# Decode kernel bound by its loads: load targets placed first in SBUF, other packet sizes, x on a second queue, one output store

## The chip, the cores and the metric

The kernel runs on one core of a Trainium2 chip; the other cores are idle. The metric is device time in microseconds (us), the median of several executions. The profile is one execution taken by the hardware profiler; its span, from the first to the last instruction, is some 1.8 us shorter than the time. SyncE and SP are the same engine, as are ScalarE and ACT, VectorE and DVE, TensorE and PE, GpSimd and POOL.

## The reference, cut to what matters

A decode step for 4 sequences: layer norm of x, an attention block over a window of 2048 cached keys and 16 key-value heads, and beside it an MLP; all are added up.

```python
xn  = layernorm(x)                                  # x: 4 x 1 x 576, bf16
q   = xn @ wq                                       # wq: 576 x 4096
o   = softmax(q @ K[window].T * 128**-0.5) @ V[window]   # K, V: 4 x 16 x 8192 x 128
out = x + o @ wo + B(xn)                            # wo: 4096 x 576
# B: x1 + gelu(layernorm(x1) @ w3) @ w4             # w3: 576 x 4608, w4: 4608 x 576
# (with one token the shifts of the first half of B give zeros, so x1 is xn; w1 and w2 are not read)
```

Only the window of K and V and the four weights have to be read: 87.17 MB. Nearly every byte is used once.

## The kernel before: what the change and the argument touch

Pools are laid out in SBUF in the order in which they are opened. All small tiles come first, the load targets after them:

```python
    const = ctx.enter_context(tc.tile_pool(name="const", bufs=1))
    small = ctx.enter_context(tc.tile_pool(name="small", bufs=2))
    kvp = ctx.enter_context(tc.tile_pool(name="kv", bufs=NKV))      # 7 tiles of 16 KB per partition, K and V
    ...                                                            # kt, pt
    wp = ctx.enter_context(tc.tile_pool(name="w", bufs=1))          # wq, then w3, then w4
    wop = ctx.enter_context(tc.tile_pool(name="wo", bufs=2))
```

The first loads, all on SyncE's queue:

```python
    x_bf = const.tile([B, D], BF16)
    nc.sync.dma_start(out=x_bf[:], in_=x2)
    wq_main = A_wq[0:KJ * P, :].rearrange("(p j) n -> p j n", j=KJ)
    for j in range(KJ):                                            # 4 DMAs, packets of 8 KB
        nc.sync.dma_start(out=wq_sb[:, j * NQ:(j + 1) * NQ], in_=wq_main[:, j, :])
```

The last load is w4, in pieces of 9, 9, 9, 5 and 4 rows per partition (a row is 1152 bytes). Everything is summed in one PSUM tile `acc`: the 576 output columns are cut in four blocks of 144, block i on partitions 32i to 32i+3 (in the code B = 4 sequences, NQD = 4 blocks, CW = 144 columns, QD = 32 partitions, D = 576, and for w4 NF = 36 rows per partition, NFH = 18). The end:

```python
    def acc_matmuls(lhsT, rhs):                                    # lhsT has 4 columns
        for i in range(NQD):
            nc.tensor.matmul(out=acc[i * QD:i * QD + B, :], lhsT=lhsT, rhs=rhs[:, i * CW:(i + 1) * CW], ...)
    ...
    fin = const.tile([P, CW], out.dtype)
    nc.vector.tensor_copy(out=fin[:], in_=acc[:])
    for i in range(NQD):
        eng = nc.sync if i % 2 == 0 else nc.scalar
        eng.dma_start(out=o2[:, i * CW:(i + 1) * CW], in_=fin[i * QD:i * QD + B, :])
```

## Time and profile before

| | before |
|---|---|
| time, median | 216.15 us (216.03 to 216.25, 3 runs) |
| span of the profile | 214.6 us |
| load queue, share of 16 DMA engines | 95.7% |
| first wq packet starts | 2.15 us |
| last data packet ends | 209.82 us |
| typical 16384-byte packet | 611 ns |

The last three rows come from the trace's record of single DMA packets (start, duration, size, queue); such numbers are called "packet records" below. They don't name the DMA engine.

From the page of the kernel before: PE's busy time, the granted TensorE clock, DMA share and rate in 40 slices of the span, and the load queue (q1) and the queue of instruction fetches (q8) with packets, MB and share of 16 engines.

```profile
PE 121.0 (56%) x2893; PEld 94.9 (44%) x2893; DVE 118.0 (55%) x223; ACT 70.1 (33%) x258; POOL 6.1 (3%) x14
PEclk9999999999999999999999999999999999999995
DMA  5999999999999999999999999999999999999960
GB/s 207 429 437 434 428 429 425 425 425 437 426 429 423 437 431 419 439 425 434 431 428 425 428 428 430 422 434 431 429 418 428 437 419 425 437 427 422 419 262 12
q1 hardware_dynamic: 7080, 87.17, 95.7%
q8 instruction: 22, 0.36, 0.6%
```

No compute engine is busy for more than 56% of the span, while DMA is at 9 tenths or more from the second slice to the 38th. The time is the stream of loads, plus what comes before its first and after its last packet. The last pieces of the chain of waits (start, duration, what) say so too: a load of w4, then the matmuls that need it, then the copy of the result.

```profile
182.78 27.43 DMA w_sb<-in_B_w_dram
210.26 0.68 PE acc L247 x16
```

The two ends in the timeline (start, duration, engine and line, operation, count, idle time before it and what ended it). At the start SyncE issues x, then wq:

```profile
0.73 0.36 SPq L87 DMA_DIRECT2D x_bf<-in_A_x_dram  x1
1.16 2.06 SPq L92 DMA_DIRECT2D wq_sb<-in_A_wq_dram  x4
...
210.26 0.65 PE L247 MATMUL acc<-w_sb,gT 128*4 128x144 bf16 x16 [0.61 <-DMA w_sb<-in_B_w_dram]
...
210.96 0.31 DVE L480 CAST fin<-acc 128x144 bf16<-128x144 f32 x1 [5.87 <-PE acc L247]
211.29 0.63 SPq L483 DMA_DIRECT2D out_dram<-fin  x2
211.30 0.92 ACTq L483 DMA_DIRECT2D out_dram<-fin  x2
```

### The profile page before, as it was taken

How to read it: one execution, taken by the hardware profiler on the slowest of the kernel's cores; microseconds unless marked ns; L12 is line 12 of the kernel's file. 1: busy time of each engine (PE TensorE's matmuls, PEld its weight loads, DVE VectorE, ACT ScalarE, POOL GpSimd, SP SyncE). 2: the span in 40 equal slices, each digit the busy share in tenths (PEclk: the TensorE clock that was granted, in tenths of full speed). 3: DMA queues.
4: the chain of work that ended last, by engine and by line, in shares of the span. 5: the costliest groups of instructions: out<-in, count | busy, mean ns of one | idle time of the engine just before them, and what ended most of it. 6: DMA issues, size and time to landing. Idle time of an engine off the chain costs nothing. (4 is left out here: it accounts for less than half of the span.)

```text
span 214.6 us, 6449 instructions
## 1 busy us (share of the span) xinstructions
PE 121.0 (56%) x2893; PEld 94.9 (44%) x2893; DVE 118.0 (55%) x223; ACT 70.1 (33%) x258; POOL 6.1 (3%) x14
## 2 busy tenths in 40 slices
PE   0461355647470017157999577677474705779752
PEld 0350143445360015145899456555453604557641
DVE  5608799766470047348610798785573924854210
ACT  0000005571634001607070045570725340709600
POOL 5400100000000000000000000000000000000000
PEclk9999999999999999999999999999999999999995
DMA  5999999999999999999999999999999999999960
GB/s 207 429 437 434 428 429 425 425 425 437 426 429 423 437 431 419 439 425 434 431 428 425 428 428 430 422 434 431 429 418 428 437 419 425 437 427 422 419 262 12
DMA packets 7123, 87.58 MB, mean 408 GB/s; under 512 B 820, under 2 KB 824, under 8 KB 1336
## 3 DMA queue, kind: packets, MB, share of 16 engines
q1 hardware_dynamic: 7080, 87.17, 95.7%
q8 instruction: 22, 0.36, 0.6%
q14 instruction: 5, 0.04, 0.0%
q10 hardware_dynamic: 16, 0.00, 0.0%
HBM read 87.17 MB, written 0.00 MB: 406 GB/s over the span
## 5 line engine op out<-in xcount | busy, mean ns | idle before, releaser
L302 ACT ACTIVATE pt<-S 32x128 bf16<-32x128 f32 x256 | 68.5, 268 | 92.0 <-issue 55.3
L259 DVE STREAM_TRANSPOSE kt<-kn 128x1024 int32<-128x1024 int32 x64 | 74.3, 1205 | 11.4 <-DMA kn<-in_A_k_cache_dram 11.4
L313 PE MATMUL O<-pt,vn 128*128 128x8 bf16 x1024 | 37.4, 169 | 43.2 <-DMA vn<-in_A_v_cache_dram 41.7
L313 PEld LDWEIGHTS <-vn 128*128 128x128 bf16 x1024 | 34.4, 105 | 51.3 <-DMA vn<-in_A_v_cache_dram 43.6
L273 PE MATMUL S<-qz,kt 128*128 128x32 bf16 x1024 | 39.1, 189 | 25.2 <-DVE kt L259 25.2
L273 PEld LDWEIGHTS <-kt 128*128 128x128 bf16 x1024 | 33.6, 106 | 36.1 <-DVE kt L259 30.4
L287 DVE TENSOR_REDUCE m<-mxT 8x1 f32<-8x128 f32 x16 | 4.4, 277 | 42.6 <-PE mxT L285 42.6
L316 PE MATMUL O<-pt,ones_bf 128*128 128x64 bf16 x128 | 17.1, 226 | 0.0
L302 ACT ACT_TABLE_LOAD x1 | 1.3, 1283 | 32.6 <-DVE mx L280 32.6
L368 PEld LDWEIGHTS <-w_sb 128*128 128x128 bf16 x144 | 11.4, 164 | 0.5 <-issue 0.4
L368 PE MATMUL AB<-ln2T,w_sb 128*128 128x4 bf16 x144 | 11.5, 202 | 0.0
L280 DVE TENSOR_REDUCE mx<-S 128x8 f32<-128x512 f32 x16 | 10.4, 652 | 1.0 <-PE S L273 1.0
L295 PE MATMUL S<-dg,ones_bf 8*128 8x512 bf16 x16 | 9.6, 601 | 0.1
L265 PE MATMUL S<-negbig,ohT 4*128 4x512 bf16 x16 | 9.6, 601 | 0.0
L316 PEld LDWEIGHTS <-ones_bf 128*128 128x128 bf16 x128 | 8.4, 104 | 0.0
L370 PE MATMUL AB<-ln2T,w_sb 128*128 128x4 bf16 x36 | 7.3, 202 | 0.0
L247 PE MATMUL acc<-w_sb,gT 128*4 128x144 bf16 x144 | 4.8, 294 | 2.8 <-DMA w_sb<-in_B_w_dram 2.8
L324 DVE TENSOR_REDUCE dn<-O 128x8 f32<-128x64 f32 x16 | 3.3, 208 | 5.5 <-PE O L316 5.5
L375 DVE COPY g_x<-AB 128x144 f32<-128x144 f32 x1 | 0.3, 307 | 10.7 <-PE AB L370 10.7
L285 PE MATMUL mxT<-ident_f,mx 128*8 128x128 f32 x16 | 6.0, 374 | 0.3 <-DVE mx L280 0.3
L370 PEld LDWEIGHTS <-w_sb 128*128 128x128 bf16 x36 | 5.9, 165 | 0.0
L247 PEld LDWEIGHTS <-gT 128*4 128x4 bf16 x144 | 3.4, 104 | 3.6 <-issue 3.5
(72 smaller groups left out, 64.9 us busy)
## 6 DMA issues: line engine op xcount, KB each, us to landing
kn<-in_A_k_cache_dram SPq DMA_DIRECT2D x16, 2048.0 KB, 29.3
vn<-in_A_v_cache_dram SPq DMA_DIRECT2D x16, 2048.0 KB, 27.0
wo_sb<-in_A_wo_dram SPq DMA_DIRECT2D x4, 1152.0 KB, 28.8
w_sb<-in_B_w_dram SPq DMA_DIRECT2D x2, 2304.0 KB, 31.8
wq_sb<-in_A_wq_dram SPq DMA_DIRECT2D x4, 1024.0 KB, 4.9
w_sb<-in_B_w_dram SPq DMA_DIRECT2D x3, 1296.0 KB, 32.8
w_sb<-in_B_w_dram SPq DMA_DIRECT2D x2, 576.0 KB, 32.2
w_sb<-in_B_w_dram SPq DMA_DIRECT2D x1, 720.0 KB
```

Source lines behind the costliest of these rows:

```text
L247: nc.tensor.matmul(out=acc[i * QD:i * QD + B, :], lhsT=lhsT, rhs=rhs[:, i * CW:(i + 1) * CW], start=False, stop=False, skip_group_check=True)
L259: nc.vector.transpose(out=kt[:], in_=src)
L265: nc.tensor.matmul(out=S_ps[h][:].rearrange("p g k j -> p (g k) j"), lhsT=ohT[:], rhs=nb, start=True, stop=False, skip_group_check=True)
L273: nc.tensor.matmul(out=S_ps[h][:, s * (SC // NQD) + g].rearrange("p k j -> p (k j)"), lhsT=kt[:, ib, g * NQD:(g + 1) * NQD, e:2 * QD:2].re ...
L280: nc.vector.reduce_max(out=mx[:], in_=S_ps[h][:].rearrange("p g k j -> p j (g k)"), axis=AX.X)
L285: nc.tensor.transpose(out=mxT[:], in_=st[h][:], identity=ident_f[:])
L295: nc.tensor.matmul(out=S_ps[h][:].rearrange("p g k j -> p (g k) j"), lhsT=ones_bf[0:NJ, :], rhs=dg, start=False, stop=False, skip_group_ch ...
L302: nc.scalar.activation(out=PT[h][kb * QD:(kb + 1) * QD, :, c4, :], in_=S_ps[h][c4 * QD:(c4 + 1) * QD, :, kb, :], func=ACT.Exp, scale=scale)
L313: nc.tensor.matmul(out=O_ps[h][:, 0:NJ], lhsT=vn[:, g * NQD + s, :], rhs=pt[:, g, s, :], start=(g == 0 and s == 0), stop=False, skip_group ...
L316: nc.tensor.matmul(out=O_ps[h][:, NJ:].rearrange("p (c j) -> p c j", j=NJ), lhsT=ones_bf[:], rhs=pt[:, g:g + DG, s, :], start=False, stop= ...
L368: nc.tensor.matmul(out=g_ps[:, i, :], lhsT=w3[:, j * F + e * (F // 2) + f0:j * F + (e + 1) * (F // 2):NFH], rhs=ln2T[:, j, :], start=False ...
L370: nc.tensor.matmul(out=g_ps[:, i, :], lhsT=w3[:, KJ * F + f0:KJ * F + F // 2:NFH], rhs=ln2T[:, KJ + e, :], start=False, stop=False, skip_g ...
```

## The change

Its intent: start the stream sooner (x on ScalarE's queue, so that wq is SyncE's first load), use larger and evenly cut packets (wq in 16 KB, w4 in even row counts), place load targets on multiples of 256 bytes, and end with one store instead of four. One store needs the 16 result rows at one partition stride, so the summing matmuls get 32 columns: the four real ones 8 apart, zeros between. The core of the diff:

```diff
+PAD = 96
+    pad = ctx.enter_context(tc.tile_pool(name="pad", bufs=1))
+    pad.tile([P, PAD], F32, name="pad")
+    (pools kv, w, wo, kt, pt opened here, then const and small)
-    nc.sync.dma_start(out=x_bf[:], in_=x2)
+    nc.scalar.dma_start(out=x_bf[:], in_=x2)
-    for j in range(KJ):
-        nc.sync.dma_start(out=wq_sb[:, j * NQ:(j + 1) * NQ], in_=wq_main[:, j, :])
+    for e in range(2):
+        lo, hi = e * 2 * NQ, (e + 1) * 2 * NQ
+        nc.sync.dma_start(out=wq_sb[:, lo:hi], in_=wq_main[:, lo:hi])
-    W4_PIECES = [0, NFH // 2, NFH, NFH + 9, NFH + 14, NF]
+    W4_PIECES = [0, 10, NFH, NFH + 10, NFH + 14, NF]
-    gT = const.tile([P, NF, B], BF16)
+    gT = const.tile([P, NF, QD], BF16)              # zero-filled; also op, in place of a small tile
-            nc.tensor.matmul(out=acc[i * QD:i * QD + B, :], lhsT=lhsT, ...
+            nc.tensor.matmul(out=acc[i * QD:(i + 1) * QD, :], lhsT=lhsT, ...
-    for i in range(NQD):
-        eng = nc.sync if i % 2 == 0 else nc.scalar
-        eng.dma_start(out=o2[:, i * CW:(i + 1) * CW], in_=fin[i * QD:i * QD + B, :])
+    nc.sync.dma_start(out=o2.rearrange("b (i n) -> i b n", i=NQD), in_=fin[0:P:RS, :])   # RS = 8
```

(The diff also moves some lines that change nothing, and lets xsum reuse the tile of xn.)

## The prediction

> **What bounds the kernel now.** DMA, end to end. The page's queue table gives queue 1 95.7% of 16 engines' span and the slices sit at 418 to 439 GB/s; PE is busy 56%. In the trace's packet records the first wq packet starts 2.15 us into the span and the last w4 packet ends at 209.8; in the chain of waits PE acc 0.68, DVE fin 0.31 and the stores follow, to 214.6. So about 207.7 of 214.6 us is one stream of 87.17 MB, and packets follow each other on an engine without gaps.
>
> **How full the stream is.** Nearly every packet of a size takes the same time: 16384 bytes 611 ns, 9216 347, 8192 309, 4608 178. That is about 8 ns plus bytes at 27.2 per ns, overlapped by 3 to 4, so a 16384-byte packet costs 607 ns. The Trainium skill, "DMA: Bandwidth & Descriptors", section "Where 436 GB/s comes from", gives 435.2 GB/s, 27.2 per engine; the slope agrees. At that rate 16384 bytes need 602 ns: alignment can win under 1%. A second loss: engines finish unevenly. Busy ones fall from 16 at 205 us to 8 at 207.5 and 4 at 209.5. Undisturbed ones end near 205.3; those hit by the 22 instruction fetches (queue 8, some 935 ns each) up to 4.5 us later. The change leaves PE's instructions, hence these fetches, alone.
>
> **What the change does.**
> 1. Alignment. The section "How a descriptor splits into AXI transactions" of the same page says a start off 256 bytes costs an extra transaction. But in the build before, all K, V, wq, w3 and wo tiles already start at multiples of 256 (256 past a multiple of 512); after, at multiples of 512. Only two w4 pieces start 128 bytes off 256. Their 10368-byte packets take the same 389 ns as those of the pieces that start on 256 (and on 512). Expected: 0, at most 1.5 us.
> 2. w4 in 10, 8, 10, 4, 4 rows: the same bytes and packets, the same last piece. 0.
> 3. x on ScalarE's queue: SP issues x at 0.73 (0.36 us) and wq only at 1.16. wq should start 0.4 us sooner, and the whole stream with it. Gain 0.4. x may land later, which only delays q, off the critical path.
> 4. wq in 16 KB packets: two of 309 become one of 611; 16 packets fewer per engine at 3.5 to 7 ns, and two issues fewer. Gain 0.1.
> 5. One store: the last store packet comes 0.7 us after the first; with one issue all come with the first. Gain 0.5.
> 6. Costs: gT and op zero-filled on POOL early, weights loaded as 32 columns instead of 4 (a load takes 104 ns for 4 and for 128 here). Off the critical path; 0.
>
> **Sum.** About 1.0 us of 216.15, all at the two ends: **215.0 us**, range **214.1 to 215.8**. Faster by over 2%: 0.02; within 2%: 0.97; slower by over 2%: 0.01.
>
> **What would show it.** First wq packet near 1.75 instead of 2.15 us. 16384-byte packets still 611 ns, slices near 428 GB/s (if alignment matters: about 605 ns and a stream 1.5 to 2 us shorter). Last data packet to end of span 4.2 us instead of 4.75. Instruction fetches still 22, engines still ending some 4 us apart.
>
> **What would make it wrong.** A 512-byte boundary counting after all; 16 KB wq issues delaying the first packet; the single store taking longer to issue; instruction fetches falling on the engines differently, each worth about 1 us at the end.

## More of the kernel before

The end of the stream by windows (from:to, length, then busy time and count of PE, PE's weight loads, DVE, ACT and POOL, granted clock, DMA share, GB/s):

```profile
207.00:208.00 1.00, 0.73 (x36) 0.58 (x36) 0.00 (x0) 0.00 (x0) 0.00 (x0) 1.00 0.53 220
208.00:209.00 1.00, 0.12 (x8) 0.12 (x11) 0.00 (x0) 0.00 (x0) 0.00 (x0) 0.88 0.41 158
209.00:210.00 1.00, 0.65 (x20) 0.44 (x13) 0.00 (x0) 0.00 (x0) 0.00 (x0) 0.50 0.18 74
```

Two things are to be seen. The stream doesn't stop at once: by 208 the DMA share is down to half, and the last packet ends at 209.82. And PE, which waits for pieces of w4 here, has only half of its clock in the last windows.

## The result, and the profile after

| | before | after |
|---|---|---|
| time, median | 216.20 us (216.03 to 216.44, 6 runs) | 215.31 us (215.11 to 215.51, 6 runs) |
| ratio | | 0.9958, 95% interval 0.9945 to 0.9971 |

It is faster by 0.4%, within the 2% called "same". Ratios here and below are the mean time of one kernel's runs over that of the kernel before in the same rounds, so they are not quite the ratio of the medians quoted.

The page after, the same lines as before:

```profile
PEclk9999999999999999999999999999999999999998
DMA  7999999999999999999999999999999999999970
GB/s 247 433 427 418 436 422 430 436 430 418 442 414 429 436 433 420 438 427 430 427 430 430 421 433 425 433 424 427 432 433 421 425 436 424 430 427 419 423 303 29
q1 hardware_dynamic: 6788, 87.17, 96.3%
q8 instruction: 22, 0.36, 0.6%
```

The middle is what it was: the same bytes, 414 to 442 GB/s, 22 instruction fetches. Only the first and the last slices differ. The chain's last pieces and the two ends in the timeline:

```profile
182.73 26.91 DMA w_sb<-in_B_w_dram
209.68 0.46 PE acc L266 x16
```

```profile
0.73 0.54 ACTq L107 DMA_DIRECT2D x_bf<-in_A_x_dram  x1
0.73 0.86 SPq L112 DMA_DIRECT2D wq_sb<-in_A_wq_dram  x2
...
209.68 0.43 PE L266 MATMUL acc<-w_sb,gT 128*32 128x144 bf16 x16 [0.91 <-DMA w_sb<-in_B_w_dram]
...
210.16 0.31 DVE L489 CAST fin<-acc 128x144 bf16<-128x144 f32 x1 [5.14 <-PE acc L266]
210.49 0.69 SPq L490 DMA_DIRECT2D out_dram<-fin  x1
```

And the windows at the end of the stream:

```profile
207.00:208.00 1.00, 1.00 (x39) 1.00 (x40) 0.00 (x0) 0.00 (x0) 0.00 (x0) 1.00 0.51 201
208.00:209.00 1.00, 0.66 (x28) 0.36 (x21) 0.00 (x0) 0.00 (x0) 0.00 (x0) 1.00 0.32 134
209.00:210.00 1.00, 0.32 (x16) 0.24 (x15) 0.00 (x0) 0.00 (x0) 0.00 (x0) 1.00 0.05 18
```

wq is now issued at 0.73 instead of 1.16. In the end PE kept its full clock, and the last 16 matmuls took 0.43 instead of 0.65 us. Put together with the packet records, in us from the start of the span (the profiled executions took 216.34 and 215.11 us, so they are 1.23 apart where the medians are 0.89 apart):

```
                                 before    after   gain so far
first wq packet starts             2.15     1.74      0.41
last data packet ends            209.82   209.36      0.46
last 16 matmuls start            210.26   209.68      0.58
result copy starts               210.96   210.16      0.80
store issued                     211.29   210.49      0.80
first store packet               212.05   211.78      0.27
last store packet ends           212.76   211.91      0.86
end of span                      214.56   213.34      1.23
```

The last column holds two surprises. The single store's first packet comes 1.29 us after its issue, where the first of four came after 0.76; so from the issue to the last packet the single store needs 1.42 us and the four needed 1.47, hardly less. And a further 0.37 us is gained after the last store packet, where neither kernel moves data any more (1.80 us before, 1.43 after).

### The profile page after: what moved, and what is told of

It is laid out like the page before. It is cut to its first block, busy times and chain, and to the rows that moved or that the text cites. A ratio compares the mean times of both kernels' runs of the same rounds, so it can differ in the third digit from the quotient of the medians.

```text
span 213.3 us, 6449 instructions
## 1 busy us (share of the span) xinstructions
PE 121.1 (57%) x2893; PEld 95.6 (45%) x2893; DVE 119.2 (56%) x223; ACT 70.4 (33%) x258; POOL 8.1 (4%) x18
## 5 line engine op out<-in xcount | busy, mean ns | idle before, releaser
L266 PE MATMUL acc<-w_sb,gT 128*32 128x144 bf16 x144 | 4.7, 298 | 1.7 <-DMA w_sb<-in_B_w_dram 1.6
L266 PEld LDWEIGHTS <-gT 128*32 128x32 bf16 x144 | 3.8, 130 | 2.4 <-issue 2.2
```

Source lines behind the costliest of these rows:

```text
L266: nc.tensor.matmul(out=acc[i * QD:(i + 1) * QD, :], lhsT=lhsT, rhs=rhs[:, i * CW:(i + 1) * CW], start=False, stop=False, skip_group_check= ...
```

## The experiments

Theories. About the loads: (A) a start address off 256 bytes costs, and the change wins nothing here only because the load targets were on such multiples before too; (A') the address doesn't matter. About the end: (E) the single store as such saves 0.4 us; (E') something else does. Kernels of one group ran on the same chip with the same runs of the kernel before. The first group's median of before was 216.32 us, the second's 216.22, the third's 216.12.

### x alone on ScalarE's queue

```diff
-    nc.sync.dma_start(out=x_bf[:], in_=x2)
+    nc.scalar.dma_start(out=x_bf[:], in_=x2)
```

> The kernel before with x alone moved to the ScalarE queue. If the earlier start of the stream is worth what the two profiles show: first wq packet near 1.74 us instead of 2.15, and 0.4 us less time than before (ratio 0.998). If the start does not matter because the end of the stream is set elsewhere: ratio 1.000.

Measured: 215.77 us, ratio 0.9975 (0.9963 to 0.9986). SyncE issues wq first now (before: at 1.16):

```profile
0.73 0.55 ACTq L87 DMA_DIRECT2D x_bf<-in_A_x_dram  x1
0.73 2.02 SPq L92 DMA_DIRECT2D wq_sb<-in_A_wq_dram  x4
```

The first wq packet came at 1.77 us, the last data packet at 209.27 (before: 2.15 and 209.82). So the earlier start goes through to the end of the stream: 0.4 us, and within the interval all of what this run gained. The Trainium skill, "DMA: Bandwidth & Descriptors", section "Issuing engines are not separate DMA queues", says that a second issuing engine saves only the sequencer's issue time, usually small. Here that time is the gain: wq is issued 0.43 us sooner and its first packet comes 0.38 us sooner, because the issue of x stood ahead of the whole stream.

### The wide columns alone, and with the single store, in the old pool order

```diff
 # wide_cols: kernel before, with
+    gT = const.tile([P, NF, QD], BF16)   # and op, idz, as in the change
-        eng.dma_start(out=o2[:, ...], in_=fin[i * QD:i * QD + B, :])
+        eng.dma_start(out=o2[:, ...], in_=fin[i * QD:(i + 1) * QD:RS, :])
 # wide_one_store: the change's single store in place of the four
```

> The kernel before with only the zero-padded 32-column weights of the accumulating matmuls; four stores as before. Theory A, the columns keep TensorE's granted clock at 1.00 in the last 5 us: the last 16 acc matmuls take 0.45 instead of 0.65 us, 0.2 us less time (ratio 0.999). Theory B, the clock at the end is an accident of each execution: no change (ratio 1.000), clock near the end 0.5 in some profiles of either kernel.

> As wide_cols, with the single store too. If the single store is worth what the prediction said, 0.5 us less than wide_cols. If its later first packet (1.29 us after the issue in the profile after, 0.76 before) eats part of it: 0.3 to 0.4 us less than wide_cols.

Measured: 219.40 us (ratio 1.0145, 1.0132 to 1.0158) and 218.54 us (1.0105, 1.0092 to 1.0118). Neither theory had that: a part of a faster kernel is 3 us slower by itself. The build shows what happened. The larger gT and op lie in the const pool, ahead of the load targets, and moved all of these from a multiple of 256 to 224 bytes past one. The packet records show the effect: the most frequent duration of a 16384-byte packet is 614 ns instead of 611 (mean without the few above 680 ns: 615.7), and an instruction fetch takes 1067 (wide_cols: 1072) instead of 935 ns. These two kernels thus became an experiment on addresses, and the next one settles it. About the clock: the last 16 matmuls took 0.67 us in both, at half clock, so the wide columns do not keep PE's clock up. About the store: in this pair the single store gains 0.86 us, more than either number of the expectation. But the four stores of wide_cols have the partition stride too; SyncE takes 1.41 us to issue its two of them, where before took 0.63. So this pair doesn't say what the single store gains over the four stores of before.

### The same with 32 unused bytes ahead of the load targets

```diff
 # wide_one_store, and at the end of the pools:
+    const.tile([P, 8], F32, name="fill")      # 32 bytes: 224 + 32 = 256
```

> wide_one_store with one change: an unused tile of 32 bytes, so that the K, V and weight tiles start at a multiple of 256 again instead of 224 bytes past one. If the start address is what made wide_one_store 2.2 us slower than before: 16384-byte packets back to 611 ns, instruction fetches back from 1070 to 930 ns, and 215.7 to 216.0 us. If the wide columns themselves slow the kernel: it stays near 218.5 us.

Measured: 216.37 us, ratio 1.0002 (0.9989 to 1.0016). Packets are back at 611 ns (mean 611.0) and fetches at 935 ns. The packets and the mean rate of the page, first wide_one_store, then wide_store_32B:

```profile
DMA packets 7111, 87.58 MB, mean 404 GB/s; under 512 B 808, under 2 KB 812, under 8 KB 1324
```

```profile
DMA packets 7111, 87.58 MB, mean 408 GB/s; under 512 B 808, under 2 KB 812, under 8 KB 1324
```

The same packets and the same bytes, 1% faster: 32 bytes nobody uses are worth 2.2 us. That is theory A. The 32 bytes also move the tiles of kt and pt, and the pad of the next runs moves every tile behind it, so no run moves load targets alone; what ties the cost to the loads is that their own packets take longer. This run says a second thing: with the addresses held, wide columns and single store together gain nothing over before.

### The changed kernel, moved off 256 bytes

```diff
-PAD = 96
+PAD = 128      # off128: all load targets 128 bytes past a multiple of 256
+PAD = 104      # off32: 32 bytes past
```

> The changed kernel with every load target moved 128 bytes off a multiple of 256. If a start off 256 costs an extra transaction of a few beats per packet: 16384-byte packets go from 611 to about 615 ns and the time rises by 1 to 2 us over the changed kernel (about 216.5 to 217). If target alignment is irrelevant: 611 ns and 215.3 us.

> The changed kernel with every load target 32 bytes past a multiple of 256. If what counts is only whether a start is on 256: like off128 or the 224 of wide_cols, 16384-byte packets at 613 to 621 ns and 217 to 218.5 us. If the cost grows with the bytes off the boundary: clearly below off128, near 215.6.

Measured: off128 217.20 us (ratio 1.0042, 1.0030 to 1.0054), off32 217.65 us (1.0063, 1.0051 to 1.0076), against 0.9958 for the change itself: 1.8 and 2.3 us slower. The records side by side:

```
load targets start       16384-byte packet, mean*   instruction fetch, mean   last data packet ends
256 past 512 (before)    611.0 ns                    935 ns                    209.82 us
on 512 (after)           611.2                       928                       209.36
32 past 256 (off32)      615.3                      1066                       211.49
128 past 256 (off128)    614.0                      1069                       211.06
224 past 256 (wide_one_store)  615.7                1067                       211.98
* without those above 680 ns: 19 to 21 that overlap an instruction fetch in time and, in after,
  off32 and off128, 16 to 18 packets of wq at the start of the stream
```

A start off 256 costs 1.8 to 2.3 us in this kernel. Whether it is on 512 or 256 past it makes no difference to a packet. An estimate from the table: one engine's share of the bytes is some 330 packets of 16 KB, and 4.1 ns on each make 1.4 us of the 2.1 us by which the stream of off32 ends later than that of after. The rest should lie with the slower fetches and the packets beside them; no run separates the two. The section "How a descriptor splits into AXI transactions" of "DMA: Bandwidth & Descriptors" counts one 32-byte beat per 32 bytes that lie between the boundary and the start, so 1, 4 and 7 beats for these three; at the 27.2 bytes per ns of these packets that is an estimate of 1.2, 4.7 and 8.2 ns. The direction agrees, the size doesn't: 4.1, 2.8 and 4.7 ns over the kernels on 256 or 512 that they derive from, and 32 bytes cost more than 128. Nor is it a fixed price: the 8192-byte wq packets of wide_one_store, 224 past 256, took the same 309 ns as in before, and off128 showed next to no excess over after from 7 to 25 us (at most 0.4 ns in any microsecond), off32 none from 7 to 18. What decides is left open; I found no relation to the compute engines' busy time in windows of 1 us.

### The store part undone

```diff
 # narrow_four: the changed kernel with 4 columns and the four stores of before
```

> The changed kernel with the store part undone (4 columns, four stores), all else kept. If the single store is a gain of its own: 0.4 us slower than the changed kernel, about 215.7. If the store gains nothing (its first packet comes 1.3 us after the issue, not 0.76) and the other parts made the gain: 215.3 us.

Measured: 216.07 us, ratio 0.9990 (0.9977 to 1.0002), 0.7 us slower than the changed kernel. Yet wide_store_32B had shown the store part to gain nothing when added to before. Two parts that don't add up point to something that they share, and the records of single instructions at the ends of the traces showed it: in every trace SyncE stands still for 0.43 to 0.48 us before its 80th recorded instruction. In the traces with 82 SyncE instructions recorded, that place falls behind the final barrier's first step, when the other engines go on with the clean-up meanwhile; in those with 83 to 86 it falls before that step, and the whole program waits.

```
                 SyncE instructions recorded    last store packet to end
before                86                         1.80 us
wide_cols             86                         1.79
x_queue               85                         1.83
wide_one_store        85                         1.89
wide_store_32B        85                         1.89
narrow_four           83                         2.09
after                 82                         1.43
off32, off128         82                         1.43, 1.43
told below: sp_plus1  83                         1.90
gather_store, more_pe 82                         1.34, 1.43
two_stores, half8     82                         1.57, 1.63
```

The place of the stall in two of these, in us from the start of the span:

```
SyncE's recorded instructions    after                           sp_plus1
79th ends                        212.55 (the barrier's first     212.73
                                 step)
80th starts                      213.02                          213.17 (the barrier's
                                                                 first step)
end of the span                  213.34                          213.97
```

The change has four DMA issues fewer on SyncE: one x, two wq, one store. On this account it is their number, not the store itself, that gained the last 0.4 us.

### One more load issue on SyncE

```diff
-    W4_PIECES = [0, 10, NFH, NFH + 10, NFH + 14, NF]
+    W4_PIECES = [0, 4, 10, NFH, NFH + 10, NFH + 14, NF]
```

> The changed kernel with the first w4 piece of 10 rows cut in pieces of 4 and 6: same bytes, SyncE's program grows from 84 to 85 instructions. In every trace so far SyncE stalls about 0.45 us before its 80th recorded instruction; programs of 85 to 88 instructions have it before the last barrier, those of 84 behind it. If that place made the 0.4 us at the end: from the last store packet to the end 1.8 to 2.1 us instead of 1.43, and 0.3 to 0.5 us more than the changed kernel (215.6 to 215.8). If the single store made it: as the changed kernel, 215.3.

(84 and 85 count the built program, of which the trace records 82 and 83.) Measured: 215.84 us, ratio 0.9984 (0.9971 to 0.9996), 0.26% of the time before, or 0.56 us, slower than the changed kernel (0.9958; compared by their ratios). The last data packet ends at 209.45 us, 0.1 later; from the last store packet to the end it takes 1.90 us. The theory holds: one load issue more on SyncE, well before the end of the program, costs 0.47 us behind the last store packet. Why SyncE stalls there, no run shows. An instruction fetch would be a guess; the packet records of all traces have none during the stall or in the 2 us before it, but one of 8192 bytes that starts 0.6 to 0.9 us after it. Whether the two belong together is open.

### The results gathered in 4 partitions, one store without a stride

```diff
-    nc.vector.tensor_copy(out=fin[:], in_=acc[:])
-    nc.sync.dma_start(out=o2.rearrange("b (i n) -> i b n", i=NQD), in_=fin[0:P:RS, :])
+    fin = const.tile([B, NQD, CW], out.dtype)        # 4 columns again in the matmuls
+    for i in range(NQD):                             # even i on VectorE, odd on ScalarE
+        copy(out=fin[:, i, :], in_=acc[i * QD:i * QD + B, :])
+    nc.sync.dma_start(out=o2, in_=fin[:].rearrange("b i n -> b (i n)"))
```

> The changed kernel with 4 columns and with the four result blocks gathered into 4 partitions by two VectorE and two ScalarE copies, then one store of 4 rows of 1152 bytes without a partition stride. If the stride of 8 partitions is what delays the single store: first store packet 0.8 us after the issue instead of 1.3, copies 0.2 us longer, about 0.3 us faster than the changed kernel (215.0). If the delay comes with any single store: 215.4.

Measured: 216.00 us, ratio 0.9984 (0.9972 to 0.9997), 0.6 us slower than the changed kernel by the ratios. The timeline of its end:

```profile
210.65 0.30 DVE L487 CAST fin<-acc 4x144 bf16<-4x144 f32 x1 [5.68 <-PE acc L261]
211.04 0.28 ACT L489 ACTIVATE fin<-acc 4x144 bf16<-4x144 f32 x1 [9.36 <-DVE fin L487]
211.35 0.30 DVE L487 CAST fin<-acc 4x144 bf16<-4x144 f32 x1 [0.41 <-ACT fin L489]
211.69 0.28 ACT L489 ACTIVATE fin<-acc 4x144 bf16<-4x144 f32 x1 [0.37 <-DVE fin L487]
212.00 0.35 SPq L490 DMA_DIRECT2D out_dram<-fin  x1
```

The four copies write one tile and were put one after the other: 1.35 us where the single copy took 0.33. That spoiled the time, but the question is answered: the store was issued at 212.00 and its first packet came at 212.77, after 0.77 us. The stores with a partition stride of 8 needed 1.29 to 1.35 us (after 1.29, wide_store_32B 1.31, wide_cols 1.35), those without it 0.75 to 0.77 (before, x_queue, narrow_four, gather_store). The stride, not the single store, makes the delay.

### A try at a better kernel: two tiles, two stores

```diff
+    fin_v, fin_a = two tiles [B, 2, CW]              # VectorE fills one, ScalarE the other
+    nc.sync.dma_start(out=o2[:, 0:2 * CW], in_=fin_v[:].rearrange("b i n -> b (i n)"))
+    nc.scalar.dma_start(out=o2[:, 2 * CW:], in_=fin_a[:].rearrange("b i n -> b (i n)"))
+    W4_PIECES = [0, NFH, NFH + 10, NFH + 16, NF]     # and o_proj before the last three pieces
```

> A try at a better kernel: the changed one with 4 columns, the results gathered in two tiles (VectorE and ScalarE, two copies each, at the same time) and stored without a partition stride by one store on each queue, w4 in pieces of 18, 10, 6 and 2 rows, SyncE again at 84 instructions. First store packet 0.8 us after the issue instead of 1.3, copies 0.3 us longer, last matmuls 0.1 to 0.2 us shorter: 214.8 us, or 215.3 if the two queues or copies hinder each other.

Measured: 215.45 us, ratio 0.9965 (0.9951 to 0.9979): no better than the change (0.9958). The end of its timeline:

```profile
208.20 2.38 PE L261 MATMUL acc<-w_sb,gT 128*4 128x144 bf16 x72
210.61 0.66 DVE L485 CAST fin_v<-acc 4x144 bf16<-4x144 f32 x2 [3.38 <-PE acc L261]
210.66 0.59 ACT L487 ACTIVATE fin_a<-acc 4x144 bf16<-4x144 f32 x2 [9.03 <-PE acc L261]
211.30 0.35 SPq L488 DMA_DIRECT2D out_dram<-fin_v  x1
```

The stores do what was wanted: issued at 211.30, packets from 212.04 to 212.24, the copies side by side in 0.66 us. But my new order of the last matmuls, a first piece of 18 rows and the attention output before the other pieces, left PE with 72 matmuls to do in a row from 208.20 on, until 210.6, while the last data packet was there at 209.45. The copy starts 0.45 us later than after, and that takes back what the stores gave. A version with the old order was not run.

### What makes the stream end unevenly

The packet records give the times at which the number of loads in flight falls: in after, 15 until 204.9 us, 8 until 207.8, the last at 209.36. The other kernels on 256 bytes look alike. Each instruction fetch takes some 930 ns, and most of them overlap a load packet of some 1100 ns instead of 611; the likely reading, since the records don't name engines, is that the two share one.

```diff
-    DG = 8
+    DG = 2        # more_pe: denominators in groups of 2: 384 more matmul pairs
```

> The changed kernel with 384 more matmul pairs on TensorE (the denominators in groups of 2 chunks instead of 8), 768 instructions more, so 25 instruction fetches of 16 KB instead of 22; same data. If the fetches set the end of the stream (22 make three on most of 8 engines, 25 make a fourth on one): the last data packet comes 1.2 to 1.5 us later, time 216.5 to 216.8. If the uneven end has another cause: last data packet near 209.4 us and 215.3 us, or somewhat more if TensorE itself falls behind.

Measured: 216.08 us, ratio 0.9995 (0.9982 to 1.0007). The fetches are 25 as foreseen:

```profile
q8 instruction: 25, 0.41, 0.7%
```

The last data packet ended at 209.37 us, as in after, not 1.2 us later. But eight loads were in flight until 209.07 instead of 207.79. So with more fetches more loads end late, while the last one stays where it was; how fetches fall on engines, and what sets the last one's end, is open. The expectation failed in its number. The time rose because PE fell behind: its last 72 matmuls ran until 210.8 us.

```diff
 # half8: two_stores, with 0.59 MB of w3 loaded through an access pattern whose outer dimension is 8
+    src8 = B_w3[0:KJ * P, 0:F // 2].rearrange("(q a j) f -> a q j f", a=8, j=KJ)[:, :, 0, :]
+    nc.sync.dma_start(out=t[:, 0:F // 2], in_=src8)
```

> two_stores with 0.59 MB of w3 arranged so that the DMA's outer dimension is 8 (the tail of wq goes to the ScalarE queue to keep SyncE at 84 instructions). If such a load runs on 8 engines, these 8 carry 2.7 us instead of 1.35, the others none. If the instruction fetches burden the other 8: last data packet 1.3 us earlier and 213.5 us. If they burden these 8, or some of both: last data packet 1.3 us later and 216.1 us. If the load spreads over 16 engines all the same: as two_stores.

Measured: 220.34 us, ratio 1.0191 (1.0177 to 1.0205), none of the three. The rate by slices shows where most of it went:

```profile
GB/s 241 431 431 428 431 428 424 431 428 428 275 338 417 430 431 424 430 428 431 428 428 431 427 424 431 428 428 425 427 430 426 428 434 428 428 428 425 407 181 7
```

Around that load (slices 11 and 12, 5.47 us each) the rate fell to 275 and 338 GB/s, against 428 an estimated 3.1 us of the 4.8 us by which the last data packet came later than in two_stores (214.2 us). By the packet records 16 packets were in flight all the while, at the height of it 8 of them from this load, so it very likely ran on few engines, as the expectation supposed (the records don't name them). But most of its 4608-byte packets (109 of 128) took 265 to 356 ns instead of 178, and those of the next load beside it some 900 ns where 13824 bytes otherwise took 516. The packets got into each other's way, though 16 were in flight; what they contend for is not shown. The run doesn't tell which engines the fetches burden: it failed as a balance and as an experiment.

## Why the prediction was right or wrong, point by point

The time was right: 215.0 foreseen with a range of 214.1 to 215.8, 215.31 measured, and "within 2%". The bound and the place of the gain, both ends of the stream, were right too. By step:

- **What bounds the kernel: right.** The middle of the stream was the same after: 611 ns per 16384-byte packet, 22 fetches, and the loads in flight thin out over the last 4.5 us of the stream.
- **1, alignment worth 0: right as a difference, and the argument had a hole.** The load targets were on 256 bytes before and after, so nothing was gained. But the prediction looked only at what could be won ("alignment can win under 1%") and read the equal 389 ns of two w4 pieces as a sign that a start off 256 is free. It isn't: 1.8 to 2.3 us in off128, off32 and wide_one_store against their aligned twins. 10368 bytes are 40.5 times 256, so a start 128 off leaves as many stretches of 256 to touch as a start on it, which may be why those packets didn't show the cost; no run tests that. (Of the two pieces that start 128 off, only one has packets of this size; the other's have 5760 bytes, 22.5 times 256. And the page that the prediction cites counts beats; an extra transaction follows from it for packets of whole multiples of 256 bytes, not for every size.)
- **3, x: right.** 0.4 foreseen; first packet at 1.74, the stream's end 0.46 earlier, and x_queue alone 0.25% faster.
- **2 and 4, w4 rows and wq packets, 0 and 0.1: not shown either way.** narrow_four holds both beside x_queue's part and was not faster than x_queue (0.9990 and 0.9975, with overlapping intervals), so any gain is below what these runs resolve. Nor do the packet records show one: by 8 us x_queue had moved 2.35 MB of loads, narrow_four 2.28 and after 2.32. The stream starts slowly with either size: the first 16 packets or so took 0.4 to 1.3 us of 8 KB each in x_queue and 0.8 to 1.6 us of 16 KB each in after and narrow_four, where the prediction counted on 309 and 611 ns.
- **5, one store, 0.5: the sum was about right, its cause was wrong.** The step that failed is "with one issue all come with the first". They do come together, but with the first 1.29 instead of 0.76 us after the issue, because the single store walks the partitions in steps of 8. From the issue to the last store packet the single store gains 0.05 us (1.42 against 1.47). What gained about 0.4 us at the end is the shorter SyncE program (sp_plus1). That the sum came near 0.5 was luck.
- **6, costs off the path, 0: right for the changed kernel, and for a reason the prediction didn't give.** The wide tiles show next to no cost in matmul time (16 of them at full clock take 0.43 us in after, 0.42 in narrow_four); but in the old pool order they would have moved every load target off 256 bytes and cost 2.2 us. The new pool order with its pad is what makes part 5 affordable. It is insurance, not a gain.
- **Not foreseen: PE's clock at the end,** worth 0.22 us in the profiled execution. In before PE waited 1.2 and 1.0 us for w4 pieces, and its clock fell at 208.76 us by the trace's clock record, near the end of the second wait and ahead of the last 36 matmuls; in after it waited 0.7 us, had 56 matmuls and waited 0.9, and the clock fell at 211.39, when PE had finished. off128, with the same code but for the pad, was at half clock again (fall at 211.15, the last 16 from 211.64 in 0.67 us), so this is no steady gain. The Trainium skill, "TensorE: Matmul & The Clock Gate", section "What's actually happening", describes a clock that falls to half after an idle window of about 3.4 us that runs freely beside the kernel. A fall that comes at another moment in each execution agrees with the free running; "idle" doesn't agree as it stands: in before PE was busy for 40% of the 3.41 us before the fall.

## What to carry to other kernels

When a kernel lives by its loads, look up the address of every load target after each change of any tile, however small: here 32 unused bytes were worth 1%. Put load targets first in SBUF, behind a pad, so that later edits can't move them. When two halves of a change don't add up, look for what they share: here it was neither half, but the number of instructions on the engine that ends the program.

## What the Trainium skill lacked or had wrong

- "DMA: Bandwidth & Descriptors", "How a descriptor splits into AXI transactions": the cost of a start off 256 bytes doesn't follow its beats. Starts 32, 128 and 224 bytes off cost 4.1, 2.8 and 4.7 ns per 16384-byte packet on average (an estimate from the page's beats and the measured 27.2 bytes per ns: 1.2, 4.7 and 8.2), and 8192-byte packets at the start of the kernel cost nothing extra (309 ns). The page doesn't give a price for a whole kernel either: 1.8 to 2.3 us of 216 here.
- No page that I found has it: instruction fetches become slower too when the loads start off 256 bytes, from 930 to 1070 ns each.
- "Runtime: NRT & Kernel Launch", "Instruction fetch mechanics", calls the cost of crossing a 16 KiB block mostly hidden. In this kernel, bound by its loads, it doesn't look hidden: 22 fetches of some 930 ns, with load packets beside them at some 1100 instead of 611 ns, and the loads in flight thin out over the last 4.5 us of the stream. With 25 fetches eight loads were in flight 1.3 us longer, though the last one ended at the same time (209.37 us).
- No page that I found has it: a store whose SBUF side steps 8 partitions has its first packet 1.29 to 1.35 us after the issue, one without a step 0.75 to 0.77 us.
- "TensorE: Matmul & The Clock Gate", "What's actually happening": the clock is said to fall after at least one idle window of about 3.4 us. In the ten traces that record a fall within reach of PE's work, PE was busy for 33 to 46% of the 3.41 us before it, and its longest idle time in that stretch was 1.3 us.
- No page that I found has it: SyncE stands still for 0.43 to 0.48 us before its 80th recorded instruction, in all the traces; one issue more on SyncE moved that stall into the end of the program and cost 0.47 us behind the last store packet (1.90 against 1.43).
- "DMA: Bandwidth & Descriptors", "Rules for kernel authors", says that an outermost dimension of c below 16 confines a DMA to at most c engines. half8, with an outer dimension of 8, had up to 8 packets of that load in flight, which agrees; but the page doesn't say that such a load also slows the engines that carry other loads: 275 and 338 GB/s in these slices instead of 428, with 16 packets in flight.
